# Splitting the last PSUM eviction and the last store of an attention and MLP kernel between two engines and two queues

## The chip, the cores and the metric

The kernel runs on one core of a Trainium2 chip. The metric is the device time of one execution in microseconds. Runs over 1.5% above the fastest run of the same kernel would be left out. The profile's span, from the first to the last instruction, is about 1.8 us shorter than the device time.

## The reference

A causal attention with a local window of 96, 8 global positions and a distance bias per head (4 batches, 8 heads, 768 positions, head size 64) is followed by an MLP with a squared ReLU:

```python
x = attn_out.transpose(0, 2, 1, 3).reshape(3072, 512)
h = x @ w_in                      # 512 -> 2048
r = np.maximum(h, 0.0)
out = (r * r) @ w_out             # 2048 -> 512, float32, 3072 rows
```

## The kernel before

The kernel makes a list of operations, orders them with a small cost model, and emits them in that order; a tile framework adds the semaphores. The 3072 rows are treated in 12 blocks of two 128-row tiles. What matters here is how the second product (`acc`) of the last block leaves: its first tile whole, its second tile in two halves of 256 columns, so that the last copy out of PSUM (the memory in which TensorE's matmuls leave these sums, `acc`) and the last store are small. The last half has a PSUM tile from a pool other than that of the rest.

```python
parts = [(0, None), (1, 0), (1, 1)] if last else [(0, None), (1, None)]
# ... for s, sub, half in order2:
    w = d_model if half is None else d_model // 2
    cols = slice(0, w) if half is None else slice(half * w, (half + 1) * w)
    own = half == 1
    def emit_s2(e, ...):
        if s == 0:
            pool, tag = (ps_g, "g") if own else (ps_acc, "acc")
            tiles["acc", blk, sub, half] = pool.tile([P, w], FP32, name="acc", tag=tag)
        hs = tiles["hs", blk, s]
        for c in range(2):
            nc.tensor.matmul(out=tiles["acc", blk, sub, half],
                             lhsT=hs[:, c, sub * P : (sub + 1) * P],
                             rhs=w_out_sb[s][:, c, cols], ...)
    # ... after the last s:
    def emit_o(e, ...):
        o_sb = work.tile([P, d_model], FP32, name="o", tag="o", bufs=NO)
        any_copy(e, o_sb[:, cols], tiles["acc", blk, sub, half])   # ScalarE for a half
    def emit_st(e, ...):
        nc.sync.dma_start(out=out[r0 : r0 + P, cols], in_=o_sb[:, cols])
# ... (cut)
```

The softmax here doesn't subtract the row's maximum and nothing guards it: scores larger than these inputs give would overflow.

## Time and profile before

| | before |
|---|---|
| device time, three runs | 212.88, 213.00, 213.36 us |
| span in the profile | 211.147 us |
| end of the last matmul | 207.909 us |
| tail: from there to the end of the span | 3.238 us |
| last store, 128 KB: issue to landing | 1.698 us |

"Issue" is the start of the DMA instruction on the engine that issues it; "landing" is the last of the 16 increments of the store's semaphore. The prediction shows and reads the lines of this profile.

### The profile page before, as it was taken

Reading aid. Unit: us, or ns where it says so; the run is one execution under the profiler, and the core shown is the slowest. Engines: PE = TensorE matmul, PEld = TensorE weight load, DVE = VectorE, ACT = ScalarE, POOL = GpSimd, SP = SyncE. Lnnn points to the kernel's source line nnn. Section 1 sums busy time; section 2 is a strip of 40 time slices with the busy share of each in tenths; the row PEclk is TensorE's granted clock in tenths of the full one; section 3 lists DMA queues with packets and bytes.
Section 4 is the critical chain, followed back from the end, with each engine's and each line's share of the span. In section 5 each row is a group of like instructions: output and inputs, shape, how many; then the busy total and the mean of one; then the engine's idle time right before and its main releaser. Section 6 shows DMA issues by size and latency. Waiting matters only on the chain.

```text
span 211.1 us, 4968 instructions
## 1 busy us (share of the span) xinstructions
PE 202.9 (96%) x1953; PEld 141.4 (67%) x1984; DVE 142.1 (67%) x368; ACT 117.5 (56%) x221; POOL 73.8 (35%) x91
## 2 busy tenths in 40 slices
PE   7998999999999999999999999999999999999993
PEld 3676877656767766666676766666666766666772
DVE  7798878523877867876786786666786876644530
ACT  6796678114846755646456466456365465533531
POOL 8997765440675029222721803604000000000000
PEclk9999999999999999999999999999999999999999
DMA  8999999999999999999999997999743123120202
GB/s 127 151 165 187 183 191 199 177 207 142 176 144 157 167 158 115 170 167 139 118 193 129 94 209 100 125 202 121 98 108 75 44 83 28 25 99 3 99 0 101
DMA packets 112615, 27.32 MB, mean 129 GB/s; under 512 B 103248, under 2 KB 109648, under 8 KB 112592
## 3 DMA queue, kind: packets, MB, share of 16 engines
q0 software_dynamic: 79200, 13.37, 85.4%
q1 hardware_dynamic: 33392, 13.64, 34.8%
q8 instruction: 15, 0.25, 0.5%
q14 instruction: 8, 0.07, 0.1%
HBM read 27.26 MB, written 6.29 MB: 159 GB/s over the span
## 4 chain that ended last, share of the span: by engine, by line
PE 87%; POOL 5%; DMA 4%; issue 1%; ACT 1%; DVE 1%; POOLq 0%
PE hT L697 39%; PE acc L767 38%; PE sc L469 5%; PE po L582 4%; DMA win<-in_moe_w_in_dram 4%; POOL qk L203 3%; POOL v L203 2%; POOL win L203 1%; ACT hr L718 1%; PE tr L386 0%; PE trx L645 0%; DVE hs L730 0%; ACT esc L515 0%; ACT o L318 0%; DVE qkT L556 0%
## 5 line engine op out<-in xcount | busy, mean ns | idle before, releaser
L718 ACT ACTIVATE hr<-hT 128x512 f32<-128x512 f32 x96 | 58.1, 605 | 75.9 <-PE hT L697 73.8
L697 PE MATMUL hT<-xT,win 128*128 128x256 bf16 x768 | 98.5, 273 | 0.9 <-ACT xT L318 0.4
L767 PE MATMUL acc<-wout,hs 128*128 128x512 bf16 (+1 forms) x369 | 94.2, 370 | 2.0 <-issue 0.6
L697 PEld LDWEIGHTS <-win 128*128 128x128 bf16 x768 | 74.5, 98 | 27.2 <-DMA win<-in_moe_w_in_dram 1.5
L730 DVE TENSOR_TENSOR hs<-hr 128x512 bf16<-128x512 f32 x96 | 65.7, 687 | 34.4 <-ACT hr L718 34.0
L767 PEld LDWEIGHTS <-hs 128*128 128x128 bf16 x400 | 35.4, 97 | 22.1
L203 POOL DMA_DIRECT2D qk<-in_q_dram x23 | 20.7, 902 | 66.4 <-DMA qkT<-qk 50.7
L515 ACT ACTIVATE esc<-sc 128x512 bf16<-128x512 f32 x78 | 41.3, 610 | 1.2 <-PE sc L469 0.6
L540 DVE TENSOR_TENSOR at<-esc,E 128x512 bf16<-128x512 bf16 x78 | 31.9, 422 | 4.1 <-ACT esc L515 2.1
L203 POOL DMA_DIRECT2D v<-in_v_dram x24 | 21.8, 910 | 1.4 <-DMA win<-in_moe_w_in_dram 1.0
L610 DVE TENSOR_TENSOR x<-po,rs 128x256 bf16<-128x256 f32 x48 | 20.4, 424 | 1.7
L203 POOL DMA_DIRECT2D qk<-in_k_dram x23 | 20.7, 902 | 0.5 <-DMA win<-in_moe_w_in_dram 0.5
L582 PEld LDWEIGHTS <-at 128*128 128x128 bf16 x352 | 15.9, 98 | 6.3 <-ACT at L515 0.7
L582 PE MATMUL po<-v,at 128*128 128x65 bf16 x352 | 17.8, 193 | 0.5 <-ACT at L515 0.3
L318 ACT COPY o<-acc 128x512 f32<-128x512 f32 (+1 forms) x17 | 9.3, 564 | 8.1 <-PE acc L767 7.6
L469 PEld LDWEIGHTS <-qkT 64*128 64x128 bf16 x352 | 10.0, 94 | 5.6 <-issue 4.4
L609 DVE RECIPROCAL rs<-po 128x4 f32<-128x4 f32 x48 | 8.8, 183 | 6.8 <-PE po L582 6.1
L469 PE MATMUL sc<-qkT 64*128 64x128 bf16 x192 | 13.2, 219 | 0.0
L469 PE MATMUL sc<-qkT,qkT 64*128 64x128 bf16 x160 | 11.4, 216 | 0.0
L556 DVE COPY qkT<-qkT 128x32 bf16<-128x32 bf16 x16 | 4.0, 251 | 9.0 <-PE sc L469 8.9
L203 POOL DMA_DIRECT2D win<-in_moe_w_in_dram x8 | 6.2, 804 | 1.7 <-DMA win<-in_moe_w_in_dram 1.2
L320 DVE COPY o<-acc 128x512 f32<-128x512 f32 x8 | 5.5, 691 | 1.7 <-PE acc L767 1.6
(41 smaller groups left out, 62.8 us busy)
## 6 DMA issues: line engine op xcount, KB each, us to landing
out_dram<-o SPq DMA_DIRECT2D x23, 256.0 KB, 2.7
v<-in_v_dram POOLq DMA_DIRECT2D x24, 128.0 KB, 6.1
qk<-in_q_dram POOLq DMA_DIRECT2D x23, 128.0 KB, 4.6
qk<-in_k_dram POOLq DMA_DIRECT2D x23, 128.0 KB, 5.3
win<-in_moe_w_in_dram POOLq DMA_DIRECT2D x8, 256.0 KB, 8.1
wout<-in_moe_w_out_dram POOLq DMA_DIRECT2D x8, 256.0 KB, 9.2
qkT<-qk SPq DMA_TRANSPOSE x18, 5.7
plain<-in_q_dram SPq DMA_DIRECT2D x1, 256.0 KB, 3.3
```

The lines of the kernel that those rows point to most:

```text
L203: nc.gpsimd.dma_start(out=dst, in_=src)
L318: nc.scalar.copy(dst, src)
L469: nc.tensor.matmul(out=tiles["sc", j, odd, g][:, at, :], lhsT=qkT[(j - kt) % NKT][half, 1, pair, :], rhs=qkT[j % NKT][half, 0, pair, :], s ...
L515: nc.scalar.activation(out=esc, in_=tiles.pop(("sc", j, odd, g)).rearrange("p a c -> p (a c)"), func=Act.Exp, scale=scale,)
L540: nc.vector.tensor_mul(at, tiles.pop(("esc", j, odd, g)), bias)
L582: nc.tensor.matmul(out=po[:, hi, :], lhsT=tiles["at", j, odd, g][:, at * P : (at + 1) * P], rhs=v_sb[kj][:, h, :], start=(i == 0), stop=(i ...
L609: nc.vector.reciprocal(rs, po[:, :, D : D + 1])
L610: nc.vector.tensor_tensor(out=x[:, 4 * hf : 4 * hf + 4, :], in0=po[:, :, :D], in1=rs.to_broadcast([P, 4, D]), op=Alu.mult,)
L697: nc.tensor.matmul(out=hT[:, c, :], lhsT=w_in_sb[s][:, kt, c * P : (c + 1) * P], rhs=tiles["xT", blk][:, kt, :], start=(kt == 0), stop=(kt ...
L718: nc.scalar.activation(hr, tiles.pop(("hT", blk, s)), Act.Relu)
L730: nc.vector.tensor_mul(hs, hr, hr)
L767: nc.tensor.matmul(out=tiles["acc", blk, sub, half], lhsT=hs[:, c, sub * P : (sub + 1) * P], rhs=w_out_sb[s][:, c, cols], start=(s == 0 an ...
```

## The change

The intent: the last 128 by 256 sums leave PSUM by ScalarE and VectorE at the same time, 128 columns each, and each half of them is stored through a queue of its own, ScalarE's and SyncE's. Below, "quarter" means these 128 columns: a quarter of a 512-column row.

```diff
+                    if half == 1:
+                        acc = tiles["acc", blk, sub, half]
+                        r0, c, m = (blk * 2 + sub) * P, cols.start, w // 2
+                        nc.scalar.copy(o_sb[:, c : c + m], acc[:, :m])
+                        nc.vector.tensor_copy(o_sb[:, c + m : c + w], acc[:, m:w])
+                        nc.scalar.dma_start(
+                            out=out[r0 : r0 + P, c : c + m], in_=o_sb[:, c : c + m]
+                        )
+                        nc.sync.dma_start(
+                            out=out[r0 : r0 + P, c + m : c + w], in_=o_sb[:, c + m : c + w]
+                        )
+                        return
                     any_copy(e, o_sb[:, cols], tiles["acc", blk, sub, half])
...
                 def emit_st(e, blk=blk, sub=sub, half=half, cols=cols):
+                    if half == 1:
+                        return
```

More of the change, by code (lines that the diff above doesn't have):

```diff
@@ L786, with emit_o @@
                 ousers = []
-                def emit_o(e, blk=blk, sub=sub, half=half, cols=cols):
+                def emit_o(e, blk=blk, sub=sub, half=half, cols=cols, w=w):
                     o_sb = work.tile([P, d_model], FP32, name="o", tag="o", bufs=NO)
+                    if half == 1:
[10 more added lines that the diff above has]
+                        return
                     any_copy(e, o_sb[:, cols], tiles["acc", blk, sub, half])
```

## The prediction

> **What bounds the kernel now.** I read the page from the top. Part 1 says whether an engine is the limit of the whole, part 4 which work the end hangs on.
>
> ```profile
> PE 202.9 (96%) x1953; PEld 141.4 (67%) x1984; DVE 142.1 (67%) x368; ACT 117.5 (56%) x221; POOL 73.8 (35%) x91
> ...
> PE 87%; POOL 5%; DMA 4%; issue 1%; ACT 1%; DVE 1%; POOLq 0%
> ```
>
> TensorE is busy for 202.9 of 211.1 us and makes up 87% of the chain that ended last. The change does not touch it. What the change touches is the stretch after the last matmul, so next I read the order of time from 208 us to the end.
>
> ```profile
> start us, us, engine line op out<-in xcount [idle before <-releaser]
> 207.95 0.37 ACT L318 COPY o<-acc 128x256 f32<-128x256 f32 x1 [1.37 <-PE acc L767]
> 208.34 0.33 SPq L802 DMA_DIRECT2D out_dram<-o  x1
> ```
>
> That is all the program's own work there: one ScalarE copy of 256 columns out of PSUM, released by TensorE, and one store of 128 rows by 1 KB issued by SyncE. The rest is waiting, as the windows show (columns: stretch, its length, then busy time of PE, PEld, DVE, ACT, POOL, the clock, the DMA share and GB/s).
>
> ```profile
> 207.90:208.34 0.44, 0.01 (x1) 0.00 (x0) 0.00 (x0) 0.37 (x1) 0.00 (x0) 1.00 0.06 21
> 208.34:209.10 0.76, 0.00 (x0) 0.00 (x0) 0.00 (x0) 0.00 (x0) 0.00 (x0) 1.00 0.00 0
> 209.10:209.70 0.60, 0.00 (x0) 0.00 (x0) 0.00 (x0) 0.00 (x0) 0.00 (x0) 1.00 0.66 219
> 209.70:210.06 0.36, 0.00 (x0) 0.00 (x0) 0.00 (x0) 0.00 (x0) 0.00 (x0) 1.00 0.00 0
> 210.06:211.10 1.04, 0.00 (x0) 0.00 (x0) 0.00 (x0) 0.00 (x0) 0.00 (x0) 1.00 0.00 0
> ```
>
> So the tail is 3.2 us: 0.44 eviction and hand-overs, 0.76 from issue to the first packet, 0.60 in which data flow, 0.36 until the receipt is seen, and 1.04 of closing waits and barriers. Only the first and the third can shrink by this change: together 1.04 us, 0.5% of the time. A gain of 2% (4.3 us) is out of reach whatever happens.
>
> The costs of single items come from the groups by form and from the last store alone (its landing view, for the stretch from 208.4 us).
>
> ```profile
> L318 ACT COPY o<-acc 128x512 f32<-128x512 f32 x15 | 8.5, 589 | 6.2 <-PE acc L767 5.7
> L320 DVE COPY o<-acc 128x512 f32<-128x512 f32 x8 | 5.5, 691 | 1.7 <-PE acc L767 1.6
> L318 ACT COPY o<-acc 128x256 f32<-128x256 f32 x2 | 0.7, 374 | 1.9 <-PE acc L767 1.9
> ...
> DMA to landing us min/median/max: 1.7/1.7/1.7
> ```
>
> ScalarE's copy costs 589 ns for 512 columns and 374 for 256, so 0.84 ns a column and 159 ns fixed. VectorE's costs 691 ns for 512.
>
> [...]
>
> **The change part by part.** The orders of instructions of the two built programs differ only at the end: TensorE's is the same, ScalarE's 256-column copy becomes one of 128 columns followed by a DMA issue, VectorE gains one 128-column copy as its last work, and SyncE's last store shrinks to 128 columns. What decides is the list of waits. VectorE's new copy does not wait for TensorE. Apart from long-fulfilled ones it waits for ScalarE's counter, at the value that ScalarE's own 128-column copy brings it to. So the framework has ordered the two copies one after the other, and "at the same time" does not happen. I take the diff's intent as void and work with the chain TensorE, ScalarE copy, VectorE copy, SyncE store.
>
> Removed from the path: the 374 ns copy. Added, as estimates from the rows above:
> - ScalarE copy of 128 columns: 159 + 128 x 0.84 = 267 ns.
> - Hand-over from ScalarE to VectorE: 31 ns, the median gap between a ScalarE end and the start of the squaring that waited for it in this trace.
> [...]
> - Hand-over to SyncE: 25 ns, as today (copy end 208.319, issue 208.344).
>
> [...]
>
> Against this stands a smaller last store. In the packet records one packet of this queue takes 86 ns with 2 KB, 48 with 1 KB and 18 with 256 B, so about 28 ns with 512 B. Each of 16 engines moves 8 rows: 8 x (48 - 28) = 0.16 us saved. The landings check this: the last full store took 2.02 us and the last half 1.70, a difference of 0.32 for 8 x (86 - 48) = 0.30. So I expect 1.54 us for the quarter, and a landing at 208.56 + 1.54 = 210.10, against 210.04 today. The ScalarE store of the other quarter is issued at about 208.25, right after its copy; by the same 0.8 us to the first packet and some 0.37 us of data (0.22 plus the 0.15 by which the engines start apart) it is done with data at about 209.4, when SyncE's begins. The two hardly meet, and ScalarE's lands at about 209.8, hidden.
>
> Last, SyncE ends the program with a row of waits on DMA counters, some 60 ns apart. Today the last store uses the fifth counter of that row, so the fifth wait and three behind it come after the landing. In the changed build SyncE's last store uses the sixth: one wait fewer, -0.06 us.
>
> Sum: +0.22 - 0.16 - 0.06 = 0.00 us. From the 213.0 us of before I predict 213.0.
>
> **The rivals.** (1) The copies do run side by side. For it: the intent. Against: the wait list. [...] (2) ScalarE's first DMA issue costs something new, a slow start of its queue or a longer way to the first packet, and lands after SyncE's. ScalarE issues 0.31 us earlier than SyncE, so it has that much slack; SyncE's issues last from 332 to 531 ns, which fits inside. For it: no trace here has a DMA from ScalarE. It would take +0.3 beyond the slack: up to 213.3 us. (3) The small packets save nothing: the store takes 1.70 us whatever its size below 128 KB, because most of it is the way to the first packet and the receipt. Then only +0.22 - 0.06 is left, 213.2 us. The step of 0.32 us between the two larger sizes speaks against it.
>
> **Range and chances.** All cases lie between 212.7 and 213.3. The three runs of before spread from 212.88 to 213.36, by 0.5 us, more than any effect here; a median of some runs of the new one may sit 0.2 off. An instruction fetch can also fall beside a store: in this trace one of 16 engines reported the next to last store 0.37 us after the others. So 212.6 to 213.5. Faster or slower by over 2% would take 4.3 us, more than the whole 3.2 us tail, and nothing ahead of the tail moves: within 2% at 0.99, half a per cent for each side.
>
> **What would show it.** In the trace of after: a VectorE copy of 128x128 that starts about 0.03 us after the end of ScalarE's[...]; a ScalarE copy of about 267; SyncE's last issue about 0.6 us after the end of the last matmul, against 0.43 now; its landing in about 1.5 us; ScalarE's store landed before it; TensorE busy 202.9 as before. Copies that overlap show the reading of the wait list wrong. A landing of 1.7 us is rival 3, a ScalarE store that lands last is rival 2. A time more than 1 us off would mean that something ahead of the last matmul moved, which I say it does not.

With the term for VectorE's 128-column copy, and with 0.267 us for ScalarE's copy and 0.031 and 0.025 for the hand-overs, SyncE's issue came to 208.56 us instead of 208.344, later by 0.22: this is the +0.22 of the forecast's sum, which came to +0.22 - 0.16 - 0.06 = 0.00 and so to 213.0 us. For rival 1 SyncE's issue came to 208.26, 0.08 earlier, and the whole to -0.07 us (212.9 us) if the two stores' packets meet and to -0.3 (212.7 us) if they do not. The 0.3 us beyond the slack in rival 2 was assumed, not worked out from a trace.

What the traces show of these terms: VectorE's 128-column copy took 292 ns in after and 291 in no_scalar_store; a packet of 512 B took 28 ns (median) in both queues of after, as the forecast had interpolated. As for the fetch in its range, the trace of before has one instruction packet of 8 KB from 207.35 to 207.91 us, while the next to last store, issued at 206.60, was under way; that it delayed the store's last increment is the author's reading.

## The result, and the profile after

Ratios here are the mean time of one kernel's runs over the mean of the other's in the same rounds, so they are not quite the ratios of the medians quoted beside them. In the first comparison the changed kernel took 213.43 us (median of 6, 212.95 to 214.31) against 212.80 (median of 6, 212.41 to 213.36): ratio 1.0034, 95% interval 1.0009 to 1.0058. That is within 2%, as forecast, but it is a loss, and 1.0034 times 213.0 is 213.7 us, outside the range of 212.6 to 213.5. (The plain median, 213.43, lies inside the range, but the kernel before ran at 212.80 in the same rounds, not at 213.0.)

The order of time in the changed kernel's tail, in the columns of the prediction's second fence:

```profile
208.27 0.27 ACT L794 COPY o<-acc 128x128 f32<-128x128 f32 x1 [1.37 <-PE acc L767]
208.57 0.51 ACTq L796 DMA_DIRECT2D out_dram<-o  x1
208.57 0.29 DVE L795 COPY o<-acc 128x128 f32<-128x128 f32 x1 [4.20 <-ACT o L794]
208.89 0.33 SPq L799 DMA_DIRECT2D out_dram<-o  x1
```

VectorE's copy starts at 208.57, after ScalarE's has run from 208.27 for 0.27 us; its bracket names ScalarE's copy, not TensorE, as what ended its wait. So the copies are in series, and SyncE issues 0.65 us after the last matmul (208.235), where it issued 0.44 after it before. Two things are new against the old order: ScalarE's DMA issue lasts 0.51 us, not 0.33, and the stores follow each other by 0.32 us.

The windows of the changed kernel, cut at its own turning points (last matmul, SyncE's issue, first packet of either store, last packet, landing seen), in the columns of the prediction's third fence:

```profile
208.23:208.89 0.66, 0.01 (x1) 0.00 (x0) 0.29 (x1) 0.27 (x1) 0.00 (x0) 1.00 0.03 8
208.89:209.57 0.68, 0.00 (x0) 0.00 (x0) 0.00 (x0) 0.00 (x0) 0.00 (x0) 1.00 0.00 0
209.57:210.18 0.61, 0.00 (x0) 0.00 (x0) 0.00 (x0) 0.00 (x0) 0.00 (x0) 1.00 0.78 215
210.18:210.60 0.42, 0.00 (x0) 0.00 (x0) 0.00 (x0) 0.00 (x0) 0.00 (x0) 1.00 0.00 0
210.60:211.63 1.03, 0.00 (x0) 0.00 (x0) 0.00 (x0) 0.00 (x0) 0.00 (x0) 1.00 0.00 0
```

Copies and hand-overs grew from 0.44 to 0.66 us. The data stretch is 0.61 us as before (0.60), although SyncE's store is half as large: it now holds the packets of two stores. The sum is 3.40 us against 3.24, so the tail accounts for 0.16 us.

But the span grew by 0.49 us (211.632 - 211.147). The other 0.33 us is there before the tail begins: the last matmul ends at 208.235 and not at 207.909. Followed back, the chain of waits shows where. In the kernel before (start, length, what):

```profile
12.39 7.84 DMA win<-in_moe_w_in_dram
20.28 1.05 PE hT L697 x8
```

and in the changed one:

```profile
12.43 8.10 DMA win<-in_moe_w_in_dram
20.58 1.05 PE hT L697 x8
```

The last of the first weights lands 0.3 us later (12.43 + 8.10 = 20.53 instead of 20.23), so the first product starts at 20.58 instead of 20.28, and TensorE, busy for 202.8 us of the span (202.9 before), carries that to the end: its last 40 matmuls on the chain start at 203.01 instead of 202.69. The instructions up to there are the same in both kernels. Whether that is chance or some effect of a program that uses one more queue had to be tested.

### The profile page after: what moved, and what is told of

The parts are those of the page before. It is cut to its first block, busy times and chain, and to the rows that moved or that the text cites. A ratio compares the mean times of both kernels' runs of the same rounds, so it can differ in the third digit from the quotient of the medians.

```text
span 211.6 us, 4972 instructions
## 1 busy us (share of the span) xinstructions
PE 202.8 (96%) x1953; PEld 141.2 (67%) x1984; DVE 142.6 (67%) x369; ACT 117.4 (55%) x221; POOL 73.8 (35%) x91
## 4 chain that ended last, share of the span: by engine, by line
PE 85%; POOL 5%; DMA 4%; DVE 1%; issue 1%; ACT 1%; POOLq 0%
PE hT L697 38%; PE acc L767 38%; PE sc L469 5%; PE po L582 4%; DMA win<-in_moe_w_in_dram 4%; POOL qk L203 3%; POOL v L203 2%; POOL win L203 1%; ACT hr L718 1%; PE tr L386 0%; DVE v L627 0%; PE trx L645 0%; DVE hs L730 0%; DVE o L320 0%; ACT esc L515 0%
```

## The experiments

Two questions: (1) is the 0.3 us at the start chance, or a price of ScalarE's queue? (2) why did SyncE's quarter store land in 1.70 us and not in the 1.54 of the prediction? The theory was that the two stores disturb each other; the rivals were that a small store costs 1.70 whatever its size, and later that ScalarE's way is slow by itself.

All tails below are from one profile each. Times from the end of the last matmul, in us:

| kernel | last matmul at | SyncE issues | ScalarE issues | last landing | landing to end | tail |
|---|---|---|---|---|---|---|
| before | 207.909 | 0.435 | - | 2.133 | 1.105 | 3.238 |
| before_again | 208.214 | 0.436 | - | 2.140 | 1.081 | 3.221 |
| after | 208.235 | 0.654 | 0.332 | 2.353 | 1.044 | 3.397 |
| after_again | 208.188 | 0.656 | 0.334 | 2.350 | 1.029 | 3.379 |
| after_third | 208.341 | 0.654 | 0.333 | 2.461 | 1.044 | 3.505 |
| one_copy_two_queues | 207.779 | 0.435 | 0.439 | 2.219 | 1.105 | 3.324 |
| two_copies_one_store | 207.536 | 0.655 | - | 2.364 | 1.081 | 3.445 |
| no_scalar_store | 208.654 | 0.651 | - | 2.211 | 1.106 | 3.317 |
| both_stores_sync | 207.651 | 0.328, 0.752 | - | 2.438 | 1.021 | 3.459 |
| two_banks_one_o | 207.547 | 0.355 | 0.276 | 2.141 | 1.106 | 3.247 |
| store_by_scalar | 208.000 | - | 0.439 | 2.328 | 1.105 | 3.433 |
| narrow_last | 208.103 | 0.329 | - | 1.912 | 1.082 | 2.994 |
| narrow_last_again | 207.894 | 0.328 | - | 1.912 | 1.081 | 2.993 |
| narrow_last_counter | 207.740 | 0.328 | - | 1.902 | 0.908 | 2.810 |

The last stores, split with the packet records (us):

| store | issue lasts | issue to first packet | its packets | last packet to landing | together |
|---|---|---|---|---|---|
| before, SyncE, 128 KB alone | 0.332 | 0.825 | 0.522 | 0.351 | 1.698 |
| store_by_scalar, ScalarE, 128 KB alone | 0.521 | 1.014 | 0.528 | 0.347 | 1.889 |
| no_scalar_store, SyncE, 64 KB alone | 0.333 | 0.831 | 0.366 | 0.363 | 1.560 |
| one_copy_two_queues, SyncE, 64 KB | 0.332 | 0.824 | 0.402 | 0.347 | 1.573 |
| one_copy_two_queues, ScalarE, 64 KB | 0.403 | 1.033 | 0.395 | 0.352 | 1.780 |
| after, ScalarE, 64 KB | 0.512 | 1.009 | 0.402 | 0.350 | 1.761 |
| after, SyncE, 64 KB | 0.332 | 0.889 | 0.398 | 0.412 | 1.699 |
| both_stores_sync, SyncE, first 64 KB | 0.332 | 0.826 | 0.362 | 0.373 | 1.561 |
| both_stores_sync, SyncE, second 64 KB | 0.383 | 0.875 | 0.367 | 0.444 | 1.686 |

"Together" is the sum of the three stretches after the first column; the issue lies inside "issue to first packet".

### The unchanged and the changed kernel once more: before_again, after_again, after_third

No edit.

> The unchanged kernel against itself, to see what chance alone does. Tail = from the modelled end of the last matmul to the end of the span, 3.24 us in the first trace (211.147 - 207.909). Both theories: tail 3.24 us again, last store 1.70 us, ratio 1.000 with an interval of some 0.003 to each side. Theory 'chance': the end of the last matmul, 207.9 us before and 208.2 after, moves from run to run by some tenths of a us because the first loads land earlier or later; so it may come out anywhere from 207.7 to 208.4 here. Rival 'ScalarE queue burdens the start': it stays near 207.9, as no DMA is issued by ScalarE here.

> The changed kernel unchanged. Both theories: tail 3.40 us again (211.632 - 208.235), made of 0.65 to SyncE's issue, 1.70 to its landing and 1.04 to the end. Theory 'chance': only the tail's +0.16 us is real, so the ratio is about 1.001 and the last matmul ends anywhere from 207.7 to 208.4. Rival 'ScalarE queue burdens the start': the last matmul ends at 208.2 or later again, and the ratio is 1.002 to 1.004 again.

> The changed kernel once more, for the size of its effect on the time alone: 1.0034 in the first comparison, 0.9997 in the second. Theory 'the first was chance in the loads at the start plus 0.16 us of tail': ratio 1.0008 with an interval of some 0.003 to each side, tail 3.38 to 3.40. Rival 'the change really costs 0.3%': ratio near 1.003 with an interval that excludes 1.

Measured: before_again 212.90 us (6 runs, 212.36 to 213.22), ratio 0.999 (0.9964 to 1.0017). after_again 212.95 us (6 runs), ratio 0.9997 (0.9972 to 1.0023). after_third 213.53 us (6 runs), ratio 1.0009 (0.9982 to 1.0035).

The chain of waits of before_again has the late load too:

```profile
12.48 8.05 DMA win<-in_moe_w_in_dram
20.58 1.05 PE hT L697 x8
```

That is the start of the changed kernel, 20.58, in a kernel that issues no DMA from ScalarE; its last matmul ends at 208.214, where the changed one has 208.235. And one_copy_two_queues, which has ScalarE's queue, ends its last matmul at 207.779. Over all profiles in the table that moment lies between 207.536 and 208.654, with and without the queue in no order. So the 0.3 us of the first comparison came from the loads at the start, which differ from execution to execution. They are not the only loads that do: in after_again the first product starts at 20.06, 0.5 us earlier than in the first trace of the changed kernel, but a transposing load (qkT) that stands on its chain from 68.94 for 8.51 us takes the gain back, and its last matmul ends at 208.188 all the same. That all three traces of the changed kernel end it at 208.19 to 208.34 therefore has more than one cause. The mean of the three ratios is 1.0013; 0.16 us of tail alone would be 1.0008. The time can't tell these apart, nor rule out a start effect of a tenth of a per cent; the tails can be compared directly, because each was measured from the last matmul. They came out at 3.38 to 3.51 us against 3.22 to 3.24.

after_third missed its expected tail (3.38 to 3.40) by 0.1 us: there ScalarE's issue lasted 0.603 us and SyncE's store took 1.807.

### The stores' part alone: one_copy_two_queues

```diff
-   nc.scalar.copy(o_sb[:, c : c + m], acc[:, :m])
-   nc.vector.tensor_copy(o_sb[:, c + m : c + w], acc[:, m:w])
+   nc.scalar.copy(o_sb[:, c : c + w], acc)
```

> The stores' part of the change alone: one ScalarE copy of 256 columns as before, then one quarter stored by ScalarE and one by SyncE. Theory 'the two stores disturb each other': SyncE issues 0.43 us after the last matmul as before; both stores' packets are on the engines at once, so a landing takes 1.75 to 1.85 us and not the 1.54 of my sum for a quarter alone; tail 3.25 to 3.35. Rival 'a store below 128 KB costs 1.70 us whatever its size': SyncE's landing 1.70 as before; ScalarE's no later; tail 3.18. Rival 'sizes add as predicted': 1.54, tail 3.02. On the start: 'ScalarE queue' says last matmul at 208.2, 'chance' says anywhere.

Measured: 212.94 us (6 runs), ratio 1.0001 (0.9973 to 1.0029); tail 3.324, as the first theory had it, but by another way. Order of time:

```profile
207.81 0.37 ACT L794 COPY o<-acc 128x256 f32<-128x256 f32 x1 [1.37 <-PE acc L767]
208.21 0.33 SPq L798 DMA_DIRECT2D out_dram<-o  x1
208.22 0.40 ACTq L795 DMA_DIRECT2D out_dram<-o  x1
```

The two issues start 4 ns apart. SyncE's store is nearly undisturbed (1.573 us); ScalarE's starts its packets 0.21 us behind and lands last (1.780). That misses what I had expected of SyncE's store (1.75 to 1.85): here the store whose packets came first nearly kept its pace (1.573 against 1.560 alone), and the later one set the end. But the later one was hardly slower than in the changed kernel, where it came first (1.780 against 1.761), although the two stores' packets overlap for about half their time. The rival of 1.70 whatever the size falls here: a quarter took 1.57.

### The copies' part alone: two_copies_one_store

```diff
-   nc.scalar.dma_start(out=out[r0 : r0 + P, c : c + m], in_=o_sb[:, c : c + m])
-   nc.sync.dma_start(out=out[r0 : r0 + P, c + m : c + w], in_=o_sb[:, c + m : c + w])
+   nc.sync.dma_start(out=out[r0 : r0 + P, c : c + w], in_=o_sb[:, c : c + w])
```

> The copies' part of the change alone: ScalarE and VectorE copy 128 columns each, then SyncE stores all 256 columns in one DMA. Theory: the VectorE copy starts 0.03 us after ScalarE's ends; SyncE issues 0.65 us after the last matmul (before 0.43), the store takes 1.70 us as before, then 1.10 us: tail 3.46, the worst of all. 'ScalarE queue burdens the start' says the last matmul ends near 207.9, as ScalarE issues no DMA; 'chance' says anywhere from 207.7 to 208.4. Ratio about 1.001.

Measured: 213.07 us (6 runs), ratio 0.9999 (0.9974 to 1.0023); issue at 0.655, store 1.709, tail 3.445. All as expected: splitting the copy cost 0.22 us here (0.655 - 0.436), because the two halves were read one after the other.

### A quarter with no other store beside it: no_scalar_store

```diff
-   nc.scalar.dma_start(out=out[r0 : r0 + P, c : c + m], in_=o_sb[:, c : c + m])
```

The result is wrong: 128 columns are never written.

> The changed kernel without ScalarE's store: both copies stay, SyncE stores its quarter, the other quarter is never stored, so the result is wrong on purpose. It measures a quarter's store with no other beside it. Theory 'the two stores disturb each other': SyncE issues 0.65 us after the last matmul, and its landing falls from the 1.70 of the changed kernel to the 1.54 of my sum (0.82 to the first packet, 0.36 of packets, 0.35 to the receipt); with the last store back on the fifth counter and so 1.10 us to the end the tail is 3.30. Rival 'a store below 128 KB costs 1.70 whatever its size': landing 1.70 here too, tail 3.45.

Measured (one look): tail 3.317; the store took 1.560 us. Windows, cut as those of the changed kernel:

```profile
208.65:209.31 0.66, 0.00 (x1) 0.00 (x0) 0.29 (x1) 0.27 (x1) 0.00 (x0) 1.00 0.03 11
209.31:210.13 0.82, 0.00 (x0) 0.00 (x0) 0.00 (x0) 0.00 (x0) 0.00 (x0) 1.00 0.00 0
210.13:210.51 0.38, 0.00 (x0) 0.00 (x0) 0.00 (x0) 0.00 (x0) 0.00 (x0) 1.00 0.61 173
210.51:210.87 0.36, 0.00 (x0) 0.00 (x0) 0.00 (x0) 0.00 (x0) 0.00 (x0) 1.00 0.00 0
210.87:211.97 1.10, 0.00 (x0) 0.00 (x0) 0.00 (x0) 0.00 (x0) 0.00 (x0) 1.00 0.00 0
```

With ScalarE's store gone the data stretch is 0.38 us instead of 0.61 (which held both stores), and the sum of the prediction for a lone quarter (1.54) holds to 0.02 us. So the presence of ScalarE's store is what took the 0.14 us from SyncE's. The split table shows where: 0.06 before the first packet, 0.03 in the packets, 0.05 behind the last one. Most of it is not in the stretch in which data flow.

### Both quarters from SyncE: both_stores_sync

```diff
-   nc.scalar.dma_start(out=out[r0 : r0 + P, c : c + m], in_=o_sb[:, c : c + m])
+   nc.sync.dma_start(out=out[r0 : r0 + P, c : c + m], in_=o_sb[:, c : c + m])
```

> The changed kernel with both quarters stored by SyncE, one after the other, no queue of ScalarE's. The first is issued at 0.33 us after the last matmul and occupies SyncE for 0.33 to 0.38, so the second goes out at 0.70 to 0.75 instead of 0.65. Theory 'two issuers disturb each other': in one queue the second's packets follow the first's without a late start, so it lands in 1.54 to 1.60; tail 3.27 to 3.37, a little better than the changed kernel's 3.39. Rival 'nearness of two stores costs, whoever issues': 1.70 again, tail 3.45. Time: the same as before within the noise.

Measured: 213.00 us (6 runs), ratio 1.000 (0.9973 to 1.0027); the first store took 1.561, the second 1.686; tail 3.459.

```profile
207.98 0.33 SPq L796 DMA_DIRECT2D out_dram<-o  x1
208.40 0.38 SPq L799 DMA_DIRECT2D out_dram<-o  x1
```

My theory that it takes two issuers falls, and the rival holds: the store that followed 0.42 us behind another paid 0.13 us in one queue, where the one 0.32 us behind paid 0.14 in two (the changed kernel). And the packets of the two did not meet here. By the packet records the first store's end at 1.516 us after the last matmul and the second's begin at 1.627, and they take 0.367 us, like a lone store's (0.366). The price was 0.05 before the first packet, where the issue was 0.05 longer, and 0.08 from the last packet to the landing. Why these two stretches grew is open. In narrow_last, below, the gap between the issues is 0.68 us and the last store took 1.58.

### ScalarE alone: store_by_scalar

The kernel before with its last half stored by ScalarE.

```diff
+   q = nc.scalar if half == 1 else nc.sync
-   nc.sync.dma_start(
+   q.dma_start(
        out=out[r0 : r0 + P, cols], in_=tiles.pop(("o", blk, sub, half))[:, cols])
```

> The kernel before, with its last half (256 columns, one ScalarE copy) stored by ScalarE in place of SyncE, no other store near it. It asks why ScalarE's quarter needed 1.01 us from issue to first packet in the changed kernel, against SyncE's 0.82 in the kernel before. Theory 'ScalarE's way is slower by itself' (its first DMA of the program): issue 0.5 us long, first packet 1.0 us after it, landing 1.88 in place of 1.70, tail 3.41. Rival 'only two issuers side by side are slow': issue 0.33, first packet 0.82, landing 1.70, tail 3.23 as before.

Measured: 213.26 us (4 runs), ratio 1.001 (0.9977 to 1.0043); tail 3.433.

```profile
208.04 0.37 ACT L318 COPY o<-acc 128x256 f32<-128x256 f32 x1 [1.38 <-PE acc L767]
208.44 0.52 ACTq L803 DMA_DIRECT2D out_dram<-o  x1
```

With no other store beside it, the same 128 KB took ScalarE 1.889 us against SyncE's 1.698, all of the difference ahead of the first packet (1.014 against 0.825). It is the length of the issue (0.521 against 0.332): from the end of the issue to the first packet both took 0.493. So ScalarE's way was slower by itself here. Whether that is so for each of its DMAs or only for the first of a program is open: every kernel here has just one.

### The change as it was meant: two_banks_one_o

The two quarters are summed in two PSUM tiles ("banks"), so that nothing orders the two copies.

```diff
+   if own:
+       tiles["acc2", blk, sub, half] = pool.tile([P, w], FP32, name="acc2", tag=tag)
...
+   for n, a in enumerate(("acc", "acc2")):
+       nc.tensor.matmul(out=tiles[a, blk, sub, half][:, :m], ...,
+           rhs=w_out_sb[s][:, c, cols.start + n * m : cols.start + (n + 1) * m], ...)
...
-   nc.vector.tensor_copy(o_sb[:, c + m : c + w], acc[:, m:w])
+   nc.vector.tensor_copy(o_sb[:, c + m : c + w], tiles["acc2", blk, sub, half][:, :m])
```

> The change as it was meant: the two quarters are summed in two PSUM banks (32 matmuls of 128 columns, by 55 ns each, in place of 16 of 256 by 109, so the same TensorE time), ScalarE reads one bank and VectorE the other. In the built program VectorE's copy then waits for TensorE alone. Theory: both copies start within 0.1 us of the last matmul and overlap; ScalarE issues at about 0.28, SyncE at 0.35 us after it (before 0.44). Stores as in the run with one copy and two queues: SyncE's takes 1.57, ScalarE's 1.76 to 1.85 and ends last, at 2.05 to 2.15, on the fifth counter with 1.10 behind it: tail 3.15 to 3.25 against 3.23 before, so even the change as meant is worth 0.1 us at most. Rival 'parallel copies are what was missing': tail 3.0 or less.

Order of time:

```profile
207.53 0.27 ACT L809 COPY o<-acc 128x128 f32<-128x128 f32 x1 [1.36 <-PE acc L772]
207.58 0.29 DVE L810 COPY o<-acc 128x128 f32<-128x128 f32 x1 [3.94 <-PE acc L772]
207.82 0.54 ACTq L811 DMA_DIRECT2D out_dram<-o  x1
207.90 0.33 SPq L814 DMA_DIRECT2D out_dram<-o  x1
```

Now the copies overlap (starts at 207.53 and 207.58), and both brackets name TensorE. The 32 matmuls of 128 columns took 1.95 us from the first start to the last end; with 0.22 us for a single one (narrow_last_counter) that is an estimated 56 ns from start to start, against the 55 expected. In before, those of 256 columns start 109 ns apart. The output tile is still one, so it was the shared PSUM tile, not the shared output tile, that put them in series. Yet the tail is 3.247 us, no better than the 3.22 to 3.24 of the kernel before: SyncE's store lands at 1.925, but ScalarE's takes 1.865 us and lands at 2.141, where the single store landed at 2.133. What the copies gave, ScalarE's queue took. (Two PSUM tiles with a single store by SyncE were not run; with its issue at 0.355 instead of 0.435 some 0.08 us might be left, an estimate.) The timed runs, 213.66 us (6 runs), ratio 1.0028 (0.9996 to 1.0059), are no better either. In three of the six the device time exceeds the span by 2.5 to 2.8 us instead of 1.8 (in the profiled one of these 213.35 us against a span of 210.8); the cause of that is open.

### A narrower last piece: narrow_last, narrow_last_again, narrow_last_counter

Cutting the last tile 384 and 128 makes the last copy and store small with one engine and one queue. The third kernel also issues three full stores in mid-program as two halves each, so that the last store falls on the eighth of the DMA counters.

```diff
-   w = d_model if half is None else d_model // 2
-   cols = slice(0, w) if half is None else slice(half * w, (half + 1) * w)
+   cols = slice(*{None: (0, d_model), 0: (0, 3 * P), 1: (3 * P, d_model)}[half])
+   w = cols.stop - cols.start
# narrow_last_counter, in emit_st as well:
+   two = blk in (7, 8, 9) and sub == 0
+   for cs in (slice(0, m), slice(m, 2 * m)) if two else (cols,):
+       nc.sync.dma_start(out=out[r0 : r0 + P, cs], in_=o_sb[:, cs])
```

> Another way to a short tail, with one engine and one queue: the kernel before with the last tile's columns cut 384 and 128 in place of 256 and 256, so that the last copy (ScalarE) and the last store (SyncE) carry 128 columns. Copy 267 ns, issue at 0.33 us after the last matmul, store 1.54 to 1.6 (the 384-column store is issued some 0.65 us ahead of it, its packets are nearly done), end 1.10 behind it: tail 2.97 to 3.05 against 3.23, gain 0.2 us, ratio about 0.999, which the timed runs can't resolve. Rival 'a store below 128 KB costs 1.70 whatever its size': tail 3.13.

> The 384 and 128 column cut again: tail 2.99 us as in its first run (before 3.22 to 3.24), ratio 0.999. Taken with the first run the time may show a gain of 0.1%; one run alone can't resolve it.

> The same cut, and in addition three full stores in mid-program (blocks 7, 8, 9) are issued as two halves, so that the last store falls on the eighth and last of the DMA counters in SyncE's closing row of waits. Three waits of 60 ns then no longer come after the landing. Theory 'each wait of the closing row behind the landing costs 0.06 us': from the landing to the end of the span 0.92 instead of 1.10, tail 2.81. Rival 'the row is hidden behind the other engines' barrier': tail 2.99. The middle of the program should not notice three more issues; ratio 0.998.

Measured: narrow_last 212.62 us (6 runs), ratio 0.9985 (0.9956 to 1.0013), tail 2.994; narrow_last_again 212.67 us (6 runs), ratio 0.998 (0.9956 to 1.0005), tail 2.993; narrow_last_counter 212.64 us (6 runs), ratio 0.998 (0.9953 to 1.0007), tail 2.810. In narrow_last the tail of the program's own work is one line in the order of time:

```profile
208.14 0.27 ACT L318 COPY o<-acc 128x128 f32<-128x128 f32 x1 [0.41 <-PE acc L767]
```

The tails are shorter than the kernel's before by 0.24 and by 0.43 us, as expected in both steps: 0.908 us from the landing to the end instead of 1.081 is 0.06 for each of three waits less. The step from 256 to 128 columns gains 0.11 us up to the issue and 0.11 in the store, which took 1.58 us although a store of 192 KB was issued 0.68 ahead of it. All three ratios lie below 1, and none is resolved from it. These are the best versions by their tails; by the time alone they count as the same.

## Why the prediction was right or wrong

- **Right: no 2% in it.** The change touches only the tail, TensorE's busy time is the same (202.8 and 202.9 us), and the time is the same within 2%.
- **Right: the copies are in series.** The wait list of the built program showed it, and the trace agrees: ScalarE 265 ns (predicted 267), gap 33 (31), VectorE 292, then 27 (25). SyncE's issue is later by 0.654 - 0.435 = 0.22 us, as predicted. two_copies_one_store shows this alone, and two_banks_one_o, where the copies of two PSUM tiles start 0.05 us apart, shows the shared PSUM tile to be the cause (whether the tile as such counts or its place in PSUM is not told apart).
- **Right: one closing wait less.** From landing to end 1.044 instead of 1.105. Over all profiles it is 1.08 to 1.11 us with the last store on the fifth counter and 1.02 to 1.04 with it on the sixth; narrow_last_counter confirms 0.06 us for each.
- **Wrong: the last store.** The step that failed is "by the same 0.8 us to the first packet ... The two hardly meet": from it the prediction gave SyncE's store the 1.54 us of a lone one. It measured 1.70. Two things were otherwise. First, ScalarE's store needed 1.01 us to its first packet, not 0.82, even with no other store beside it (store_by_scalar). Its packets therefore ran from 1.34 to 1.74 us after the last matmul instead of ending where SyncE's begin, and SyncE's, from 1.54 to 1.94, met them for half their length. Second, not to meet would not have made it free: the prediction let the neighbour act on the data alone and held the way to the first packet and the receipt fixed, but 0.11 of the 0.14 us over the lone 1.56 lie in these two, and in both_stores_sync a store paid 0.13 us without meeting. Whether SyncE's store would have been faster had ScalarE's been on time is not shown, and why these stretches were longer beside a near store is open. The term for the smaller size was itself well sized (1.56 in no_scalar_store); what it gave was taken by the nearness of the other store. The sum was +0.22 - 0.16 - 0.06 = 0; measured it is +0.22 + 0.00 - 0.06 = +0.16.
- **Rivals.** Rival 3 (a small store saves nothing) describes the landing that came, 1.70, but is wrong as a cause: a lone quarter took 1.56. Rival 2 was right that ScalarE's DMA had a longer way to its first packet, by 0.19 us; that fitted in the slack, so its store did not land last in the changed kernel (2.093 against 2.353 us after the last matmul), but it pushed its packets into the time of SyncE's. Rival 1, run as two_banks_one_o, came out at a gain of nothing, not the 0.07 us that I gave it.
- **Wrong: the range.** I took the noise from three runs, which spread over 0.5 us. In the later comparisons the kernel before itself ran from 212.4 to 214.6 us. Its two profiles differ by 0.3 us in when the first loads land; the slowest runs were not profiled, so the cause of the rest isn't shown. The forecast that "nothing ahead of the tail moves" was true of the program and not of the executions. The first ratio of 1.0034 was mostly this, so it was mostly chance that the range was left: two more comparisons gave 0.9997 and 1.0009. A comparison of six runs leaves some 0.5 us to each side (the first interval is 0.0049 wide, 1.0 us). Around a point 0.16 us higher that gives 212.7 to 213.7 us, whose upper end is where the measured time lies.

## What to carry to other kernels

Look at the wait list of the built program before you count on two engines at once: in this kernel two reads of one PSUM tile were ordered one after the other (starts 0.30 us apart in the changed kernel), and a tile for each cured it (0.05 us in two_banks_one_o). At the end of a program count the way of a store (issue, first packet, receipt) and the waits behind it, not only copies and bytes: in these runs another store 0.32 to 0.42 us ahead, which cost the last one 0.13 to 0.14 us, or a store from ScalarE, whose only DMA had its first packet 0.19 us later than SyncE's, took back what splitting gave. Making the last piece itself smaller (narrow_last) shortened the tail by 0.24 us where splitting it lengthened it by 0.16. When an effect is below the spread of the runs, measure the stretch that changed from a common event in each trace.
